# A gated feed-forward kernel whose first x transfers carry one block of 128 columns, whose first matmuls run in halves of 256 tokens, and whose last output piece has 128 columns

## Chip, cores and metric

The kernel runs on one core of a Trainium2 chip. The metric is the time of one execution in microseconds (us) of device time. The profile's own span is about 1.8 us shorter than that time (297.4 against 299.16 us in the profiled run of the kernel before).

## The reference

```python
B, S, D, F = 32, 32, 1024, 3584            # 1024 tokens, all bf16
def reference(x, w_gate, w_up, w_down):
    return (gelu_tanh(x @ w_gate) * (x @ w_up)) @ w_down
```

A "block" below is one of the 8 slices of 128 along D, the dimension that the first two products sum over. A "pair m" is one group of 128 gate columns and 128 up columns of F. The first two products read x with D on the partitions. Of the first 512 tokens, blocks 0 and 1 of x are loaded as they are and transposed on PE. The DMA transposes blocks 2 to 7, and all blocks of the other 512 tokens, on the way.

## The kernel before: the parts that matter

A helper, `pr.add(engine, operation, ..., r=, w=)`, records every operation with the keys that it reads and writes, and makes the waits from them. All operations therefore carry one line number (L98) in the profile, and one reads by the names of the tiles.

```python
# PE: dummy matmuls while the first data is on its way
for n in [512] * 6 + [128] * 2:
    pr.add("pe", "matmul", ps[:, 3, 0:n], one[:, 0:P], one[:, 0:n], ...)
NX = 2
for i, eng in enumerate(("sp", "act")):        # x, blocks 0 and 1: rows of 512 B, 128 KB on each queue
    pr.add(eng, "dma_start", xn[:, 2*i:2*i+2, :], x_r[:, 2*i:2*i+2, 0:NX*P], w=[("xn", i)], dma=f"xn{i}")
for k in range(NX):                            # weights of blocks 0 and 1, pairs 0-3
    load_w("sp", "g", 0, k, k + 1)
    load_w("act", "u", 0, k, k + 1)
for k0, k1 in ((2, 3), (3, 4), (4, 5), (5, 6), (6, 8)):
    load_x(0, k0, k1)                          # DMA transposes, on SP
load_w("act", "g", 0, 2, 4)                    # weights of blocks 2 and 3
load_w("act", "u", 0, 2, 4)
# ... (cut)
for k in range(NX):                            # eight transposes and four copies, before any real matmul
    for i, b in enumerate((6, 7) if k == 0 else (4, 5)):
        half = ps[:, b, 0:P].bitcast(BF16)
        for t in range(2):
            pr.add("pe", "transpose", half[:, t*P:(t+1)*P], xn[:, 2*i+t, k*P:(k+1)*P], ident[:, :], ...)
        pr.add("dve", "tensor_copy", xT[:, k, i*256:(i+1)*256], half, ...)
# ... (cut) then for tokens 0-511: per block k, four gate and four up matmuls of 512 tokens,
#     pair m into PSUM banks 2m (gate) and 2m+1 (up)
# ... (cut) the output, in pieces of (token chunk, column, columns), each copied by ACT or DVE in turn
jobs = [[(tc, 0, 512), (tc, 512, 512)] for tc in range(TC - 1)]
jobs += [[(TC-1, 0, 512)], [(TC-1, 512, 256)], [(TC-1, 768, 256)]]
```

## Time and profile before

| | before |
|---|---|
| time, median of the 3 runs first given | 300.06 us (299.55 to 300.38) |
| span of the profile | 297.4 us |
| PE busy | 292.7 us, 98% |
| first real matmul | 4.61 us |
| block 1's first matmul | 6.33 us |
| last copy out of PSUM starts | 294.96 us |

These are lines from the profile page of the kernel before: the busy time of each engine with its share of the span, and the chain of waits that ended last, by engine.

```profile
PE 292.7 (98%) x1362; PEld 79.3 (27%) x808; DVE 42.5 (14%) x68; ACT 37.5 (13%) x67; POOL 0.7 (0%) x6
PE 98%; issue 0%; ACT 0%
```

PE is the bound, and nearly the whole chain is PE. Little can therefore be won, apart from what happens before PE starts (4.6 us) and after it stops (2.4 us).

This is the timeline of the kernel before at its start. The columns are the start in us, the length of the stretch in us, engine, line, operation, output<-inputs, forms and count. A bracket, where there is one, gives the idle time just before and what ended it.

```profile
3.51 1.06 PE L98 MATMUL ps<-ident,xn 128*128 128x128 bf16 x8
3.96 0.93 DVE L98 COPY xT<-ps 128x256 bf16<-128x256 bf16 x4 [3.96 <-PE ps L98]
4.61 1.02 PE L98 MATMUL ps<-xT,wg 128*128 128x512 bf16 x4
...
6.33 1.03 PE L98 MATMUL ps<-xT,wg 128*128 128x512 bf16 x4
```

Transposes at 3.51 us, copies at 3.96, the first matmul at 4.61. From there a matmul starts every 0.216 us, so eight of them, one block, take 1.73 us. Block 1 starts at 6.33 and block 2 at 8.06 (not shown), without a gap. Before a certain moment PE runs at half this rate: the dummies of 512 columns start 0.427 us apart. That moment is called the clock step below. Here it lies between the last transpose (starts at 4.25, the transposes 0.106 us apart) and the first matmul: the clock record of this trace begins at 4.59 us.

These are the early transfers of the kernel before (output<-input, issuing queue, kind, count, KB, us from issue to landing). The first two were issued at 0.74 us, the third (block 0's gate weights) at 1.26, the fourth (block 1's gate weights) at 1.75, and the last (up weights of blocks 2 and 3) at 2.76.

```profile
xn<-in_x_dram ACTq DMA_DIRECT2D x1, 128.0 KB, 2.9
xn<-in_x_dram SPq DMA_DIRECT2D x1, 128.0 KB, 2.7
wg<-in_w_gate_dram SPq DMA_DIRECT2D x1, 128.0 KB, 2.7
wg<-in_w_gate_dram SPq DMA_DIRECT2D x1, 128.0 KB, 3.8
wu<-in_w_up_dram ACTq DMA_DIRECT2D x1, 256.0 KB, 5.8
```

So x is there at 3.40 and 3.62 us, block 0's gate weights at 4.01 and block 1's at 5.51. (The prediction's 3.44, 3.64 and 3.96 are what the rounded durations give.) The up weights of blocks 2 and 3 are there at 8.60 us; PE uses them at 8.93. This is a supply that keeps just ahead of PE, with 0.3 to 1.3 us to spare for the weights of blocks 0 to 2 and for x of block 2.

These are the shares of the chain of waits of the kernel before within its first 18 us, by line.

```profile
by line: PE ps L98 96.0%; issue 0.8%
```

No DMA stands in it. And this is the end of the kernel before, in the timeline:

```profile
294.96 0.38 ACT L98 ACTIVATE xT<-ps 128x256 bf16<-128x256 f32 x1 [5.52 <-PE ps L98]
295.37 0.33 SPq L98 DMA_DIRECT2D out_dram<-xT  x1
```

The last copy takes 0.38 us for 256 columns. Then comes the issue of the store, and the span ends at 297.38: 2.42 us after the start of that copy.

### The profile page before, as it was taken

To read this page: it belongs to the slowest core of one execution; us is meant where nothing else is said; L and a number is where in the kernel's file an instruction comes from. 1 tells how busy PE (TensorE), PEld (TensorE's weight loads), DVE (VectorE), ACT (ScalarE), POOL (GpSimd) and SP (SyncE) were. 2 spreads that over 40 slices of the span, in tenths; PEclk is the share of its full clock that TensorE was granted. 3 is DMA by queue.
4 is the path that set the end of the run, shared out by engine and by line. 5 is a ranking of instruction groups with operands and counts; after the bars stand their busy time and mean duration, and the time that the engine had idled before them with its cause. 6 is when DMAs were issued, how large, how long until landed. Compare 5 with 4: busy or idle time off the path is not lost.

```text
span 297.4 us, 2549 instructions
## 1 busy us (share of the span) xinstructions
PE 292.7 (98%) x1362; PEld 79.3 (27%) x808; DVE 42.5 (14%) x68; ACT 37.5 (13%) x67; POOL 0.7 (0%) x6
## 2 busy tenths in 40 slices
PE   8999999999999999999999999999999999999996
PEld 4444222222222222222222222222222222222255
DVE  1030311112211111111111221110000000000000
ACT  1030411111111111211111111110000000000010
POOL 0000000000000000000000000000000000000000
PEclk9999999999999999999999999999999999999999
DMA  7999734006608309121030030000101101001011
GB/s 201 268 247 354 237 106 142 1 0 225 198 2 304 121 10 355 62 102 39 0 141 2 0 141 0 0 2 0 35 0 37 35 0 35 15 23 35 0 35 35
DMA packets 28842, 26.37 MB, mean 89 GB/s; under 512 B 8224, under 2 KB 25248, under 8 KB 28832
## 3 DMA queue, kind: packets, MB, share of 16 engines
q1 hardware_dynamic: 26640, 24.25, 25.5%
q10 hardware_dynamic: 2192, 1.97, 2.3%
q8 instruction: 8, 0.13, 0.2%
q14 instruction: 2, 0.02, 0.0%
HBM read 22.28 MB, written 2.10 MB: 82 GB/s over the span
## 4 chain that ended last, share of the span: by engine, by line
PE 98%; issue 0%; ACT 0%
PE ps L98 56%; PE ps L163 43%; ACT xT L98 0%
## 5 line engine op out<-in xcount | busy, mean ns | idle before, releaser
L98 PE MATMUL ps<-xT,wg 128*128 128x512 bf16 x250 | 88.4, 379 | 0.3
L98 PE MATMUL ps<-xT,wu 128*128 128x512 bf16 x250 | 87.9, 379 | 0.2
L98 PE MATMUL ps<-wd,hT 128*128 128x512 bf16 (+1 forms) x272 | 83.6, 357 | 0.0
L163 PE MATMUL ps<-wd,hT 128*128 128x512 bf16 x196 | 74.3, 379 | 0.4
L163 PE MATMUL ps<-xT,wu 128*128 128x512 bf16 x189 | 71.6, 379 | 0.3
L163 PE MATMUL ps<-xT,wg 128*128 128x512 bf16 x189 | 71.6, 379 | 0.2
L98 DVE TENSOR_TENSOR hT<-g,ps 128x512 bf16<-128x512 f32 x56 | 36.3, 685 | 158.1 <-PE ps L98 152.5
L98 ACT ACTIVATE g<-ps 128x512 f32<-128x512 f32 x56 | 30.8, 595 | 159.8 <-PE ps L98 159.8
L98 PEld LDWEIGHTS ps<-wd,hT 128*128 128x128 bf16 x280 | 27.4, 98 | 69.8 <-issue 65.8
L98 PEld LDWEIGHTS ps<-xT,wu 128*128 128x128 bf16 x256 | 25.0, 98 | 71.7 <-issue 64.1
L98 PEld LDWEIGHTS ps<-xT,wg 128*128 128x128 bf16 x256 | 25.0, 98 | 71.5 <-issue 64.0
L98 DVE CAST xT<-ps 128x512 bf16<-128x512 f32 (+1 forms) x8 | 5.3, 658 | 87.7 <-ACT xT L98 79.8
L98 ACT ACTIVATE xT<-ps 128x512 bf16<-128x512 f32 (+1 forms) x9 | 5.2, 573 | 94.6 <-PE ps L98 94.6
L98 PE MATMUL ps<-const-bfloat16-1.0 128*128 128x512 bf16 (+1 forms) x8 | 2.9, 545 | 0.8 <-PEq L309 0.8
L98 ACT ACT_TABLE_LOAD x1 | 1.3, 1283 | 3.5 <-issue 3.5
L98 PEld LDWEIGHTS ps<-const-bfloat16-1.0 128*128 128x128 bf16 x8 | 1.0, 137 | 2.4 <-issue 2.4
L98 DVE COPY xT<-ps 128x256 bf16<-128x256 bf16 x4 | 0.9, 292 | 4.0 <-PE ps L98 4.0
L98 PE MATMUL ps<-ident,xn 128*128 128x128 bf16 x8 | 1.1, 311 | 0.0
L98 PEld LDWEIGHTS ps<-ident,xn 128*128 128x128 bf16 x8 | 0.8, 136 | 0.0
L98 POOL TENSOR_SCALAR_AFFINE_SELECT ident<-ident 128x128 bf16<-128x128 bf16 x1 | 0.3, 295 | 0.2 <-POOL ident L98 0.2
L98 POOL MEMSET ident<- 128x128 bf16 x1 | 0.2, 205 | 0.3 <-POOLq L309 0.3
L98 ACT ACTIVATE warm<-const-float32-0.0 128x1 f32<-128x1 f32 x1 | 0.2, 203 | 0.0
(4 smaller groups left out, 0.4 us busy)
## 6 DMA issues: line engine op xcount, KB each, us to landing
wd<-in_w_down_dram SPq DMA_DIRECT2D x7, 1024.0 KB, 5.1
wg<-in_w_gate_dram SPq DMA_DIRECT2D x6, 1024.0 KB, 7.8
wu<-in_w_up_dram SPq DMA_DIRECT2D x6, 1024.0 KB, 10.1
out_dram<-xT SPq DMA_DIRECT2D x15, 128.0 KB, 1.7
wg<-in_w_gate_dram ACTq DMA_DIRECT2D x3, 256.0 KB, 4.9
wu<-in_w_up_dram ACTq DMA_DIRECT2D x3, 256.0 KB, 5.2
wu<-in_w_up_dram ACTq DMA_DIRECT2D x2, 128.0 KB, 3.8
wg<-in_w_gate_dram SPq DMA_DIRECT2D x2, 128.0 KB, 3.3
```

The source lines that it names most:

```text
L98: ins = name(eng, *args, **kw) if callable(name) else getattr(eng, name)(*args, **kw)
L163: return eng.add_instruction(mybir.InstMatmult(start_tensor_calc=start, stop_tensor_calc=stop, ldweights=False, name=nc.get_next_instructi ...
```

## The change

The intent: PE could start sooner if its first transfer were smaller and its first matmuls needed less of x. So the first x transfers carry only block 0 (64 KB on each queue). Block 0's matmuls of pairs 0 to 2 run on the first 256 tokens while the second 256 are still being copied. Block 1 of x comes in one later transfer, and PE transposes it between two of those halves. One dummy matmul is dropped. The last output piece has 128 columns instead of 256, so that its copy and its store are shorter.

```diff
-for n in [512] * 6 + [128] * 2:
+for n in [512] * 5 + [128] * 2:
...
-    pr.add(eng, "dma_start", xn[:, 2*i:2*i+2, :], x_r[:, 2*i:2*i+2, 0:NX*P], w=[("xn", i)], dma=f"xn{i}")
-for k in range(NX):
-    load_w("sp", "g", 0, k, k + 1)
-    load_w("act", "u", 0, k, k + 1)
+    pr.add(eng, "dma_start", xn[:, 2*i:2*i+2, 0:P], x_r[:, 2*i:2*i+2, 0:P], w=[("xn", i, 0)], dma=f"xn{i}")
+load_w("sp", "g", 0, 0, 1)
+load_w("act", "u", 0, 0, 1)
+pr.add("sp", "dma_start", xn[:, :, P:NX*P], x_r[:, 0:4, P:NX*P], w=[("xn", 0, 1), ("xn", 1, 1)], dma="xn2")
+load_w("act", "g", 0, 1, 2)
+load_w("act", "u", 0, 1, 2)
...
+pe_x(0)                                   # 4 transposes, 2 copies (banks 6 and 7)
+six = [(m, kind) for kind in "gu" for m in range(3)]
+for m, kind in six:
+    mm_gu(kind, m, 0, 0, 2*m + (kind == "u"), quarter=0)     # tokens 0-255
+for m, kind in six:
+    if (m, kind) == (0, "u"):
+        pe_x(1)                           # 4 transposes, 1 copy of 512 (bank 7)
+    mm_gu(kind, m, 0, 0, 2*m + (kind == "u"), quarter=1)     # tokens 256-511
# pair 3 of block 0 follows in full; its up matmul writes bank 7
...
-jobs += [[(TC-1, 0, 512)], [(TC-1, 512, 256)], [(TC-1, 768, 256)]]
+jobs += [[(TC-1, 0, 512)], [(TC-1, 512, 384)], [(TC-1, 896, 128)]]
```

On the queues, this gives the third place on SP, where block 1's gate weights stood, to block 1 of x. The gate weights go to ACT, and everything behind them on ACT moves one issue down.

More of the change, by code (lines that the diff above doesn't have):

```diff
@@ L167, in held_matmul, with mm_gu @@
                 tile_size=(P, P), tile_position=(0, 0)))
-        def mm_gu(kind, m, h, k, bank, w=(), held=False):
+        def mm_gu(kind, m, h, k, bank, w=(), held=False, quarter=None):
             buf, slot = where[m]
             wt = (wg_b if kind == "g" else wu_b)[buf]
-            pr.add("pe", held_matmul if held else "matmul", ps[:, bank, :], wt[:, k, slot * P:(slot + 1) * P], xT[:, k, h * 512:(h + 1) * 512],
-                start=(k == 0), stop=(k == DK - 1),
-                r=[(kind, buf, slot, k), ("x", k, h)] + ([("x", k, "b")] if h == 0 else []), w=[("ps", bank), *w])
+            c0, n = (0, 512) if quarter is None else (256 * quarter, 256)
+            keys = [("x", k, h)] if quarter != 1 else []
+            if h == 0 and quarter != 0:
+                keys.append(("x", k, "b"))
+            kw = {} if h or m > 2 else dict(skip_group_check=True)
+            pr.add("pe", held_matmul if held else "matmul", ps[:, bank, c0:c0 + n],
+                   wt[:, k, slot * P:(slot + 1) * P], xT[:, k, h * 512 + c0:h * 512 + c0 + n],
+                   start=(k == 0 and quarter != 1), stop=(k == DK - 1),
+                   r=[(kind, buf, slot, k), *keys], w=[("ps", bank), *w], **kw)
         glu_n = [0]
@@ L197, in bass_standalone__geglu_ffn__sampling_kernel @@
         for i, eng in enumerate(("sp", "act")):
-            pr.add(eng, "dma_start", xn[:, 2 * i:2 * i + 2, :], x_r[:, 2 * i:2 * i + 2, 0:NX * P], w=[("xn", i)], dma=f"xn{i}")
-        for k in range(NX):
-            load_w("sp", "g", 0, k, k + 1)
-            load_w("act", "u", 0, k, k + 1)
+            pr.add(eng, "dma_start", xn[:, 2 * i:2 * i + 2, 0:P], x_r[:, 2 * i:2 * i + 2, 0:P], w=[("xn", i, 0)], dma=f"xn{i}")
+        load_w("sp", "g", 0, 0, 1)
+        load_w("act", "u", 0, 0, 1)
+        pr.add("sp", "dma_start", xn[:, :, P:NX * P], x_r[:, 0:4, P:NX * P], w=[("xn", 0, 1), ("xn", 1, 1)], dma="xn2")
+        load_w("act", "g", 0, 1, 2)
+        load_w("act", "u", 0, 1, 2)
         def load_x(h, k0, k1, r=()):
@@ L211, in bass_standalone__geglu_ffn__sampling_kernel, with pe_x @@
         pr.add("act", "activation", warm[:, 0:1], const0, ACTF.Gelu_apprx_tanh)
-        for k in range(NX):
-            for i, b in enumerate((6, 7) if k == 0 else (4, 5)):
-                half = ps[:, b, 0:P].bitcast(BF16)
+        def pe_x(k):
+            for i in range(2):
+                b = 6 + i if k == 0 else 7
+                half = ps[:, b, (0 if k == 0 else i * P):(P if k == 0 else (i + 1) * P)].bitcast(BF16)
                 for t in range(2):
                     pr.add("pe", "transpose", half[:, t * P:(t + 1) * P], xn[:, 2 * i + t, k * P:(k + 1) * P],
-                           ident[:, :], r=[("xn", i), "ident"], w=[("ps", b)])
-                pr.add("dve", "tensor_copy", xT[:, k, i * 256:(i + 1) * 256], half, r=[("ps", b)],
-                       w=[("x", k, 0) if i == 0 else ("x", k, "b")])
+                           ident[:, :], r=[("xn", i, k), "ident"], w=[("ps", b)])
+                if k == 0:
+                    pr.add("dve", "tensor_copy", xT[:, k, i * 256:(i + 1) * 256], half, r=[("ps", b)],
+                           w=[("x", k, "b") if i else ("x", k, 0)])
+            if k:
+                pr.add("dve", "tensor_copy", xT[:, k, 0:512], ps[:, 7, 0:256].bitcast(BF16), r=[("ps", 7)],
+                       w=[("x", k, 0)])
+        pe_x(0)
+        six = [(m, kind) for kind in "gu" for m in range(3)]
+        for m, kind in six:
+            mm_gu(kind, m, 0, 0, 2 * m + (kind == "u"), quarter=0)
+        for m, kind in six:
+            if (m, kind) == (0, "u"):
+                pe_x(1)
+            mm_gu(kind, m, 0, 0, 2 * m + (kind == "u"), quarter=1)
         KO = 2
@@ L226, in bass_standalone__geglu_ffn__sampling_kernel @@
                 steps += [(m, kind, k) for kind in "gu" for k in range(KO)] if h else []
-            for k in range(KO if h else 0, DK - KO):
+            if h == 0:
+                steps += [(3, kind, 0) for kind in "gu"]
+            for k in range(KO if h else 1, DK - KO):
                 steps += [(m, kind, k) for kind in "gu" for m in range(4)]
@@ L270, in bass_standalone__geglu_ffn__sampling_kernel @@
         jobs = [[(tc, 0, 512), (tc, 512, 512)] for tc in range(TC - 1)]
-        jobs += [[(TC - 1, 0, 512)], [(TC - 1, 512, 256)], [(TC - 1, 768, 256)]]
+        jobs += [[(TC - 1, 0, 512)], [(TC - 1, 512, 384)], [(TC - 1, 896, 128)]]
         ji = 0
```

## The prediction

> **What bounds the kernel now.** TensorE does. The page gives PE 292.7 us busy of a 297.4 us span (98%), and the chain of waits that ended last is 98% PE. The timeline shows the stream of 512-column matmuls starting one every 0.216 us from 4.61 us, without a gap, to about 294.9 us. Only the ends are left to win: 4.6 us of head and 2.5 us of tail.
>
> *Head (timeline and DMA view).* The two x transfers (128 KB each, issued at 0.74) land at 3.44 and 3.64 us; the dummy matmuls occupy PE until 3.51. Eight transposes follow, 0.106 us apart, four copies run at 3.96 to 4.89 us, and the first real matmul starts at 4.61, just after the second copy (end 4.46). Its weights had landed at 3.96. The dummies (0.43 us each at 512 columns) and the transposes run at half rate; the matmuls from 4.61 run at full rate. [...]
>
> *Tail.* Last matmul ends 294.9, copy on ACT 0.38 us, issue at 295.37, landing 1.6 us later.
>
> **What changes, costed.**
>
> 1. Half the bytes in the first x transfers: landing about 0.35 us earlier (estimate from the 430 KB moved by 3.44 us). One dummy fewer: PE free at about 3.1. Two, not four, transposes and one copy before the first half matmul: it starts near 4.0 us, 0.6 us earlier.
> 2. But it then runs before the clock step, at half rate: 0.5 us of it does 0.25 us of work. Loss 0.25 us.
> 3. The four transposes of block 1 and their copy move into the stream: 0.22 us of PE time. Their copy (512 columns, estimate 0.43 us from the 292 ns copies and the slope of the casts) must end before the up matmul of m=3, which uses the same PSUM bank 7. PE has 0.77 us of work from the start of these transposes, the copy chain needs about 1.0: a stall near 0.2 us. Block 1 of x lands at about 5.2 us (estimate), when PE wants it: 0 to 0.2 us more.
> 4. Halves: 0.109 us each, as the 256-column matmuls of the tail show, so no cost.
>
> Sum: block 1's matmuls start at 6.4 to 6.6 us, against 6.33 before. The head gains nothing, or loses 0.1 to 0.2 us. The weights of blocks 2 and 3, now one issue (0.47 us) later on the ACT queue, had 0.4 to 0.5 us of slack, and should just be in time.
>
> 5. Tail: the copy falls from 0.38 to 0.28 us (slope of the two ACT forms) and the landing by 0.05. Gain 0.15 us if 128-column matmuls run at 0.056 us each. If the weight load (98 ns in the records) limits them, [...]. No run here shows which.
>
> **Predicted:** 300.1 us, range 299.2 to 301.0. Faster by over 2%: 0.01, within 2%: 0.97, slower: 0.02.
>
> **Signs.** Right: first real matmul at 3.9 to 4.1 us with starts 0.21 us apart for halves at first; a PE gap before m=3's up matmul; block 1's matmuls at 6.4 to 6.6; 128-column matmuls 56 ns apart at the end. Wrong: halves at 0.108 us from the start, no gap, block 1 before 6.2.
>
> **What would make it wrong.** The clock step coming later [...]; late block-1 x or weights of blocks 2 and 3; a step before 4 us [...]; weight loads binding in the tail.

The forecast came to 300.1 us, range 299.2 to 301.0. Terms are cut from it where the mark stands, because they rested on figures that no run of this case shows: when the clock step comes and what moves it, what a step at another time would lose or gain, and what weight loads could cost in the tail. The estimate of 5.2 us for block 1 of x stands without the numbers that it came from. The terms that remain give 299.9 to 300.1 us: 300.06 before, 0 to 0.2 us lost in the head, 0.15 us gained in the tail.

## More of the kernel before

Only runs in the fast state are compared. One run in the slow state turned up and is described at the end.

## The result, and the profile after

| | before | after |
|---|---|---|
| time, median of 6 runs each | 299.99 us (299.55 to 300.54) | 300.70 us (300.04 to 301.63) |
| ratio after/before | | 1.0024, 95% interval 1.0004 to 1.0044 |
| span of the profile | 297.4 us | 298.2 us |
| first real matmul | 4.61 us | 4.31 us |
| block 1's first matmul | 6.33 us | 7.26 us |
| last copy starts | 294.96 us | 296.08 us |
| from there to the end of the span | 2.42 us | 2.17 us |

Ratios are the mean time of one kernel's fast runs over that of the other's of the same rounds, so not quite the ratio of the medians quoted. The kernel after is slower by about 0.7 us, a quarter of a per cent.

The same page lines, of the kernel after (busy times; the chain of waits by engine):

```profile
PE 294.2 (99%) x1393; PEld 78.0 (26%) x813; DVE 42.7 (14%) x67; ACT 37.4 (13%) x67; POOL 0.7 (0%) x6
PE 97%; DMA 1%; SPq 0%; ACT 0%; issue 0%
```

A DMA now stands in the chain. The start of the kernel after, in the timeline:

```profile
3.08 0.63 PE L98 MATMUL ps<-ident,xn 128*128 128x128 bf16 x4
3.54 0.51 DVE L98 COPY xT<-ps 128x256 bf16<-128x256 bf16 x2 [3.54 <-PE ps L98]
4.31 0.50 PE L98 MATMUL ps<-xT,wg 128*128 128x256 bf16 x3 [0.60 <-DMA wg<-in_w_gate_dram]
4.81 0.50 PE L98 MATMUL ps<-xT,wu 128*128 128x256 bf16 x3
5.15 0.49 PE L98 MATMUL ps<-xT,wg 128*128 128x256 bf16 x3
6.11 0.40 PE L98 MATMUL ps<-ident,xn 128*128 128x128 bf16 x4 [0.47 <-DMA xn<-in_x_dram]
6.34 0.49 PE L98 MATMUL ps<-xT,wu 128*128 128x256 bf16 x3
6.55 0.42 DVE L98 COPY xT<-ps 128x512 bf16<-128x512 bf16 x1 [2.50 <-PE ps L98]
7.03 0.39 PE L98 MATMUL ps<-xT,wu 128*128 128x512 bf16 x1
7.26 1.03 PE L98 MATMUL ps<-xT,wg 128*128 128x512 bf16 x4
```

PE starts 0.30 us earlier. Three groups of halves follow, the last of which starts at 5.15 us. At about 5.48 PE has issued the last of them (three, 0.109 us apart). The next thing in its order are block 1's transposes, which start at 6.11: PE stood still for 0.63 us. (The bracket gives less, since it counts from the modelled end of the last matmul.) Then the up matmul of pair 3 comes at 7.03, 0.36 us after the matmul before it instead of 0.216: it waited for the copy at 6.55 to leave bank 7. Block 1 begins at 7.26, 0.93 us later than before.

Waits of the kernel after in its first 16 us (engine, tiles <- what it waited for: us in total, times, longest; PEld is PE's loading of weights); before, no such line names a DMA.

```profile
PEld ps L98 <- DMA wu<-in_w_up_dram: 1.1, 3, 0.5
PE ps L98 <- DMA wg<-in_w_gate_dram: 0.6, 1, 0.6
PE ps L98 <- DMA xn<-in_x_dram: 0.5, 1, 0.5
```

And the chain of waits of the kernel after in its first 18 us, first by line, then the piece that matters (start, us, what):

```profile
by line: PE ps L98 67.2%; DMA xn<-in_x_dram 24.0%; SPq L98 5.0%; issue 1.2%
1.75 4.32 DMA xn<-in_x_dram
```

The piece that decides is block 1 of x, 4.3 us under way from its issue at 1.75 us. The early transfers of the kernel after, in the same columns as before (issued at 0.74, 0.74, 1.24, 1.75 and 3.50 us):

```profile
xn<-in_x_dram ACTq DMA_DIRECT2D x1, 64.0 KB, 2.2
xn<-in_x_dram SPq DMA_DIRECT2D x1, 64.0 KB, 2.0
wg<-in_w_gate_dram SPq DMA_DIRECT2D x1, 128.0 KB, 3.0
xn<-in_x_dram SPq DMA_DIRECT2D x1, 128.0 KB, 4.3
wu<-in_w_up_dram ACTq DMA_DIRECT2D x1, 256.0 KB, 6.4
```

Block 0 of x lands at 2.74 and 2.95 us, 0.7 us earlier than x did before. Block 0's gate weights, behind half as many bytes, land no earlier in this profile, at 4.26 us (in the four other profiles of this head at 3.81 to 4.00). Block 1 of x lands at 6.06. The up weights of blocks 2 and 3 land at 9.9 instead of 8.6 us.

The end of the kernel after, in the timeline:

```profile
295.72 0.33 PE L98 MATMUL ps<-wd,hT 128*128 128x128 bf16 x3
296.08 0.28 ACT L98 ACTIVATE xT<-ps 128x128 bf16<-128x128 f32 x1 [5.52 <-PE ps L98]
296.39 0.33 SPq L98 DMA_DIRECT2D out_dram<-xT  x1
```

The last three of the 128-column matmuls start within 0.11 us (0.056 us apart), the copy takes 0.28 us, and the span ends 2.17 us after its start instead of 2.42. The tail is a gain of 0.25 us. The head lost 1.12 us (294.96 to 296.08): the first activation that reads PSUM comes at 15.60 us before and at 16.73 after, and from there to the start of the last copy 279.36 us pass in both. In 13 profiles this stretch is the same within 0.001 us, so what differs between these kernels lies before it or after it.

### The profile page after: what moved, and what is told of

It reads as the page before. It is cut to its first block, busy times and chain, and to the rows that moved or that the text cites. A ratio compares the mean times of both kernels' runs of the same rounds, so it can differ in the third digit from the quotient of the medians.

```text
span 298.2 us, 2585 instructions
## 1 busy us (share of the span) xinstructions
PE 294.2 (99%) x1393; PEld 78.0 (26%) x813; DVE 42.7 (14%) x67; ACT 37.4 (13%) x67; POOL 0.7 (0%) x6
## 2 busy tenths in 40 slices
DMA packets 29370, 26.37 MB, mean 88 GB/s; under 512 B 9392, under 2 KB 25776, under 8 KB 29360
## 4 chain that ended last, share of the span: by engine, by line
PE 97%; DMA 1%; SPq 0%; ACT 0%; issue 0%
PE ps L98 55%; PE ps L163 42%; DMA xn<-in_x_dram 1%; SPq L98 0%; ACT xT L98 0%
## 5 line engine op out<-in xcount | busy, mean ns | idle before, releaser
L98 PE MATMUL ps<-xT,wg 128*128 128x512 bf16 (+1 forms) x259 | 90.5, 377 | 0.6 <-DMA wg<-in_w_gate_dram 0.6
L98 PE MATMUL ps<-xT,wu 128*128 128x512 bf16 (+1 forms) x259 | 90.5, 377 | 0.0
L98 PE MATMUL ps<-wd,hT 128*128 128x512 bf16 (+2 forms) x280 | 86.6, 358 | 0.0
L163 PE MATMUL ps<-xT,wg 128*128 128x512 bf16 x192 | 72.8, 379 | 0.0
L163 PE MATMUL ps<-xT,wu 128*128 128x512 bf16 x192 | 72.8, 379 | 0.0
L98 PEld LDWEIGHTS ps<-wd,hT 128*128 128x128 bf16 x280 | 26.3, 98 | 71.0 <-issue 65.8
L98 DVE COPY xT<-ps 128x256 bf16<-128x256 bf16 (+1 forms) x3 | 0.9, 336 | 6.0 <-PE ps L98 6.0
```

The costliest lines, as they stand in the source:

```text
L98: ins = name(eng, *args, **kw) if callable(name) else getattr(eng, name)(*args, **kw)
L163: return eng.add_instruction(mybir.InstMatmult(start_tensor_calc=start, stop_tensor_calc=stop, ldweights=False, name=nc.get_next_instructi ...
```

## The experiments

Two theories stood against each other. **Supply**: the head is a race between PE and the transfers that feed it; the change made block 1 of x and the weights behind it later, so PE waits, whenever it starts. **Order**: the loss comes from what PE now does, halves and transposes in the stream, a copy to wait for, and half-rate work before the clock step. Twelve runs were made, in four batches: nine new kernels, the tail change alone twice more, and the kernel after once more. Each was timed in 6 executions beside 11 of the kernel before.

### The two parts of the change alone

`tail_only` is the kernel before with one line changed:

```diff
-jobs += [[(TC-1, 0, 512)], [(TC-1, 512, 256)], [(TC-1, 768, 256)]]
+jobs += [[(TC-1, 0, 512)], [(TC-1, 512, 384)], [(TC-1, 896, 128)]]
```

> The kernel before with only the last output piece changed to 384 and 128 columns. Theory: the tail part is a gain of 0.2 to 0.35 us on its own (in the profile after, 2.1 us passed from the start of the last copy to the end of the span against 2.4 before), so a ratio of 0.9990 to 0.9993; the 128-column matmuls start 0.055 us apart. Rival (weight loads bind the 128-column matmuls): [...].

Measured: 299.39 us against 299.83, ratio 0.9982 (0.9970 to 0.9995). That is more than expected, but the expected ratios lie within the interval. Starts of the 128-column matmuls: 0.056 us apart, each with its own weight load (98 ns in the records). So the weight loads do not bind there. The rival's figures are cut, since no run of this case shows them.

`head_only` is the kernel after with that line put back.

> The kernel after with the tail of before, so the head changes alone, and a second look at them. Theory: 0.9 to 1.3 us slower than before (ratio 1.003 to 1.0045), block 1 of x landing at 5.6 to 6.3 us again and PE waiting for it for 0.4 us or more. Rival (that landing was an accident of one execution): block 1 lands by 5.3 us, PE does not wait, the loss is under 0.5 us.

Measured: 301.05 us, ratio 1.0033 (1.0012 to 1.0054), so about 1.0 us lost by the head, as expected. The wait of 0.4 us or more for block 1 of x, also expected, is a miss: PE did not wait for it here. The timeline of `head_only`:

```profile
4.01 0.82 PE L98 MATMUL ps<-xT,wg 128*128 128x256 bf16 x3 [0.31 <-DMA wg<-in_w_gate_dram]
5.78 0.39 PE L98 MATMUL ps<-ident,xn 128*128 128x128 bf16 x4
6.92 1.03 PE L98 MATMUL ps<-xT,wg 128*128 128x512 bf16 x4
...
10.20 0.61 PE L98 MATMUL ps<-xT,wu 128*128 128x512 bf16 x2 [0.53 <-DMA wu<-in_w_up_dram]
```

Here PE ran at half rate from 4.01 to about 5.5 us (half matmuls 0.213 us apart) and therefore met block 1 of x (landed at 5.73) without waiting. Yet block 1's matmuls started at 6.92 us, within the 6.88 to 7.27 of the other profiles of this head. And at 10.20 the up matmuls of block 2 waited for weights that landed at 10.15. The half-rate work and the wait for x fill the same time: they do not add.

### PE's new order on the old transfers

`order_only` is the kernel after with the transfers, dummies and tail of before:

```diff
 # against the kernel after
-(x in 64 KB pieces, block 1 third on SP, block 1's gate weights on ACT; 5 dummies; 384 + 128)
+(x in 128 KB pieces of two blocks, weights alternately on SP and ACT; 6 dummies; 256 + 256)
```

> The kernel before with its own transfers and dummies, but the halves and the late transposes of block 1 as PE does them after. Theory (the loss is made of transfers): no PE wait for a DMA in the first 7 us, block 1's matmuls start at 6.3 to 6.6 us (6.33 before, 7.26 after), total within 0.3 us of before. Rival (the order of work on PE costs the microsecond): block 1's matmuls at 7 us or later and a loss near 1 us.

Measured: 299.79 us against 299.83, ratio 0.9999 (0.9984 to 1.0014). Its timeline:

```profile
4.38 0.49 PE L98 MATMUL ps<-xT,wg 128*128 128x256 bf16 x3 [0.36 <-DMA wg<-in_w_gate_dram]
5.61 0.39 PE L98 MATMUL ps<-ident,xn 128*128 128x128 bf16 x4
6.75 1.03 PE L98 MATMUL ps<-xT,wg 128*128 128x512 bf16 x4
```

Its expectation held for the time; two details missed: PE waited for block 0's gate weights (landed at 4.27 us) and again, for about 0.25 us, for its up weights (4.90), and block 1 started at 6.75, a little late. PE did not wait for block 1 of x. The order of work on PE, including the wait for bank 7 (0.14 us here too), neither gains nor costs more than the interval allows, 0.5 us. `order_only` and `head_only` ran in the same batch and differ in the transfers and one dummy alone; `six_dummies` below loses as much with the dummy put back. The microsecond comes from the transfers.

### Why block 1 of x is late

`x1_both_queues` splits block 1's transfer over both queues and puts block 1's gate weights back on SP:

```diff
-pr.add("sp", "dma_start", xn[:, :, P:NX*P], x_r[:, 0:4, P:NX*P], ...)
-load_w("act", "g", 0, 1, 2)
+for i, eng in enumerate(("sp", "act")):
+    pr.add(eng, "dma_start", xn[:, 2*i:2*i+2, P:NX*P], x_r[:, 2*i:2*i+2, P:NX*P], ...)
+load_w("sp", "g", 0, 1, 2)
```

> The kernel after, but block 1 of x is split over both queues as block 0 is, its two 64 KB transfers third on each, and block 1's gate weights are back on SP. Theory [...] block 1 lands by about 5.2 us instead of 6.05, the PE wait for it falls from about 0.6 us to under 0.2, and the time is 0.4 to 0.7 us below that of after. Rival (block 1 is late because it stands behind the first weights, or the engines are busy): it lands at 5.7 us or later and nothing is won.

Measured: block 1 landed at 4.90 and 5.08 us, and the wait for it was gone. This landing is as expected. And the time was 300.53 us, ratio 1.0016 (1.0002 to 1.0030), against 1.0024 for the kernel after in its own batch: the expected gain of 0.4 to 0.7 us does not show, and the 0.2 us between the two ratios are within the noise. The timeline of `x1_both_queues` shows where the time went:

```profile
4.95 0.46 PE L98 MATMUL ps<-ident,xn 128*128 128x128 bf16 x4
5.93 0.39 PE L98 MATMUL ps<-xT,wu 128*128 128x512 bf16 x1
7.09 1.04 PE L98 MATMUL ps<-xT,wg 128*128 128x512 bf16 x4 [0.77 <-DMA wg<-in_w_gate_dram]
...
9.80 1.02 PE L98 MATMUL ps<-xT,wg 128*128 128x512 bf16 x4 [0.81 <-DMA xT<-in_x_dram]
```

Block 0 was finished 0.18 us ahead of the kernel before: its last matmul started at 5.93, so block 1 could have begun at 6.15. Then PE stood until 7.09 for block 1's gate weights (landed at 7.04), and again until 9.80 for x of block 2 (landed at 9.66). One wait was taken away and the next in line took its place.

`x1_double` is the kernel after with twice the bytes in the late transfer, in as many packets (29370 in the whole execution with either):

```diff
-pr.add("sp", "dma_start", xn[:, :, P:NX*P], x_r[:, 0:4, P:NX*P], ...)
+pr.add("sp", "dma_start", xn[:, :, P:3*P], x_r[:, 0:4, P:3*P], ...)   # block 2 of it is not used
```

> The kernel after with the late x transfer doubled: it carries blocks 1 and 2 (rows of 512 B, 256 KB; block 2 of it is not used). The number of its packets stays, its bytes double. Theory [...]: it lands less than 0.5 us later than after's 5.7 to 6.05 us, so at 6.0 to 6.5 us. Rival [...]: twice the bytes behind the same start need another 0.8 us or more, so 6.7 us or later.

Measured: 300.21 us, ratio 1.0010 (0.9989 to 1.0031); the late transfer landed at 6.08 us, inside the expected 6.0 to 6.5 us. The transfer in its list of DMA issues:

```profile
xn<-in_x_dram SPq DMA_DIRECT2D x1, 256.0 KB, 4.3
```

It took 4.3 us for 256 KB, as after it took 4.3 us for 128 KB (3.9 to 4.3 us in four profiles). Twice the bytes move the landing by 0.4 us at most (6.08 us against 5.69 to 6.06). Each packet record in the trace is one row, and its length on an engine is (256 and 1024 B the same in the traces of before and after, 512 B in that of before):

| row of | packet record, median of the first 12 us |
|---|---|
| 256 B | 18 ns |
| 512 B | 27 ns |
| 1024 B | 46 ns |

Among the first transfers of `x1_double` only this one has rows of 512 B. Its 512 rows moved between 3.59 and 5.23 us. In that stretch SP's queue moved 684 rows in all, ACT's 182 rows of 1024 B: nearly four to one. How the two queues shared the engines, and whether ACT's queue always had rows ready, stays open, since the records do not name the engine. Of the 4.3 us, about 1.85 passed before the first row moved (the rows of block 0's gate weights, ahead on SP, ended at 3.63), 1.64 while the rows moved, and 0.85 from there to the last completion. So the forecast of the landing came true, but as an estimate of the author's: its reason was not shown.

One reading stands in the traces. The third transfer on SP lands that late with either set of transfers. With those of before it is block 1's gate weights, 128 KB in 128 rows of 1024 B. They landed at 5.51, 5.95, 5.63, 5.35 and 6.61 us in the five profiles at the head of the table further down, 5.81 on the mean. Block 1 of x in that place landed at 5.69 to 6.08, 5.87 on the mean, in 512 rows of 256 or of 512 B. The place was as late before as after. But block 1's gate weights are wanted at 6.33, and PE wants block 1 of x when it has issued the last halves before its transposes, at 5.0 to 5.5 us in the four profiles that waited.

`x_small_packets` is the kernel before, but each of its two first transfers takes one block of all four token groups, so that the same 128 KB come in rows of 256 B:

```diff
-pr.add(eng, "dma_start", xn[:, 2*i:2*i+2, :], x_r[:, 2*i:2*i+2, 0:NX*P], ...)
+pr.add(eng, "dma_start", xn[:, :, i*P:(i+1)*P], x_r[:, 0:4, i*P:(i+1)*P], ...)
 # every transpose now waits for both
```

> The kernel before with the same two first transfers of 128 KB, but each takes one block of 128 columns of all four token groups, so rows of 256 B instead of 512. Theory (a 256 B packet keeps an engine 18 ns, a 512 B one 27): x takes 64 packets of 18 ns on each engine instead of 32 of 27, lands 0.3 us later (3.7 to 3.9 us), the first real matmul starts at 4.85 to 5.0 us and the time grows by 0.2 to 0.4 us (ratio 1.0007 to 1.0013). Rival (bytes count, packets don't): x lands at 3.4 to 3.7 us as before, no loss.

Measured: x landed at 3.54 and 3.84 us (3.40 and 3.62 before, 3.50 and 3.78 in `two_halves_tail`, which has the old rows and ran in the same batch), the first matmul started at 4.99 us, and the time was 300.01 us, ratio 0.9994 (0.9972 to 1.0016). The landing moved by at most 0.2 us, less than the 0.3 expected, and no loss was seen. In `g1_on_act`, with the old rows and also in that batch, x landed at 3.64 and 3.87. Inconclusive: rows of 256 B in these two transfers cost 0.2 us of landing at most, and no time that shows.

### The other weights, and the early start

`g1_on_act` is the kernel before with block 1's gate weights issued from ACT:

```diff
-    load_w("sp", "g", 0, k, k + 1)
+    load_w("sp" if k == 0 else "act", "g", 0, k, k + 1)
```

> The kernel before with one transfer moved: block 1's gate weights are issued from ACT, so that the up weights of block 1 and the weights of blocks 2 and 3 come one issue (about 0.5 us) later on ACT, as after. Theory (the head is a race of transfers with PE, and the later weight issues lose it): PE waits for weights of blocks 1 to 3 for 0.3 to 0.8 us, ratio 1.001 to 1.003. Rival [...]: no more waits than before, ratio under 1.001.

Measured: 300.24 us, ratio 1.0008 (0.9981 to 1.0034), inconclusive in time. In its profile the up weights of blocks 2 and 3 landed at 10.34 us, 0.3 us after PE wanted them, although PE was late too, since the clock step came at 6.66 us in that execution. This run does not settle what the moved issue alone is worth, and the rival's reason is cut, since it was not shown.

`six_dummies` is the kernel after with the sixth dummy put back, which takes away the early start; `after_again` is the kernel after, unchanged, in the same batch.

> The kernel after once more, unchanged, for a second profile of it and as the measure of the next run, on the same chip. Theory: ratio to before 1.002 to 1.004 with the tail's gain in it; PE waits for block 1 of x, or comes to it late because the clock step was late; block 1's matmuls start at 6.8 to 7.3 us.

> The kernel after with the sixth dummy matmul put back, so that PE reaches the first transposes and the first half matmuls about 0.4 us later. Theory (PE only waits for block 1 of x and later weights, so the early start is worth nothing): the same time as after_again within 0.2 us, block 1's matmuls again at 6.8 to 7.3 us. Rival (the early start is worth its 0.4 us and something else lost more): 0.3 to 0.5 us slower than after_again.

Measured: `after_again` 300.29 us, ratio 1.0031 (1.0004 to 1.0059); `six_dummies` 300.56 us, ratio 1.0029 (1.0004 to 1.0053). The timeline of `six_dummies`:

```profile
4.39 0.49 PE L98 MATMUL ps<-xT,wg 128*128 128x256 bf16 x3 [0.26 <-DVE xT L98]
5.74 0.40 PE L98 MATMUL ps<-ident,xn 128*128 128x128 bf16 x4 [0.20 <-DMA xn<-in_x_dram]
6.88 0.59 PE L98 MATMUL ps<-xT,wg 128*128 128x512 bf16 x2
```

The first half matmul starts at 4.39 instead of 3.97 us, and block 1 at 6.88 instead of 6.99. By the ratios, starting 0.4 us later costs nothing that shows (each interval is 0.7 us or more to either side, so the times alone do not exclude 0.4 us). The profiles say why: PE only stands that much less before block 1 of x (landed at 5.69; 5.80 in `after_again`).

### All heads side by side

Landings are the last of the 16 completions of a transfer, and the columns are in us from the start of the span. The last column is the first activation that reads PSUM. It comes once pair 0 of all 8 blocks is done, and what follows up to the last copy takes 279.36 us in every profile, so it sums up the head. `x1_both_queues`, `g1_on_act` and `x_small_packets` have transfers of their own and are left out (first activation at 17.33, 17.14 and 17.48 us).

| profile | first matmul | block 1 of x landed | block 1 starts | up weights of blocks 2, 3 landed | first activation |
|---|---|---|---|---|---|
| *transfers of before* | | | | | |
| before | 4.61 | 3.62 | 6.33 | 8.60 | 15.60 |
| tail_only | 4.61 | 3.53 | 6.33 | 9.36 | 16.09 |
| tail_third | 4.69 | 3.52 | 6.44 | 9.19 | 16.03 |
| order_only | 4.38 | 3.36 | 6.75 | 8.78 | 16.01 |
| two_halves_tail | 4.44 | 3.78 | 6.66 | 10.07 | 17.10 |
| *transfers of after* | | | | | |
| after | 4.31 | 6.06 | 7.26 | 9.94 | 16.73 |
| after_again | 3.97 | 5.80 | 6.99 | 9.83 | 17.32 |
| head_only | 4.01 | 5.73 | 6.92 | 10.15 | 18.06 |
| six_dummies | 4.39 | 5.69 | 6.88 | 9.82 | 17.07 |
| x1_double | 4.04 | 6.08 | 7.27 | 9.85 | 16.68 |

On the mean, the first activation comes at 16.17 us in the upper group and at 17.17 in the lower: the 1.0 us that `head_only` lost in the timed runs. Block 1 starts at 6.50 and at 7.06 us, so 0.56 us of it is gone by then. In four of the five lower profiles PE waited for block 1 of x; in `head_only` half-rate matmuls filled that time. The other 0.44 us is lost later, in waits for weights and for x of the following blocks. The up weights of blocks 2 and 3 are an example. They land 0.72 us later in the lower group (9.92 against 9.20), but PE wants them 2.59 us after block 1 starts (twelve matmuls of 0.216 us) and is itself 0.56 us later. They come up to 0.6 us too late in four of the five lower profiles. In the upper group they come 0.4, 0.2 and 0.8 us too late in `tail_only`, `tail_third` and `two_halves_tail`. So the old transfers have no slack there either, and these ten profiles do not single out one later transfer as the cause of the 0.44 us. One profile of a kernel is one draw: the landing of the same transfer moves by up to 1.5 us between the profiles of one group, and the times of one kernel spread over 0.7 to 2.7 us.

### Versions meant to beat both

`two_halves_tail` keeps the old transfers and early transposes, runs only the first two gate matmuls in halves, and has the new tail. Its core:

```diff
+for half in range(2):
+    for m in range(2):
+        mm_gu("g", m, 0, 0, 2*m, half=half)      # then the other matmuls of block 0 in full
```

> A candidate: the kernel before with its transfers, dummies and early transposes, the 384 and 128 tail, and only the first two gate matmuls of block 0 in halves, so that PE starts after the first copy. Expected: first real matmul at 4.4 us instead of 4.61, no wait for a copy, time 0.3 to 0.7 us below before (ratio 0.9977 to 0.9990); if the transfers bound the head, as the theory has it, the 0.2 us of the start are lost again at blocks 1 to 3 and it equals the tail change alone (0.9982).

Measured: first matmul at 4.44 us, time 299.71 us, ratio 0.9991 (0.9969 to 1.0012). The earlier start shows in the profile, but no gain over the tail alone.

The tail alone ran twice more.

> The tail change alone once more. Theory: 0.2 to 0.6 us below before again (ratio 0.998 to 0.9993); from the start of the last copy to the end of the span 2.05 to 2.2 us against 2.4. Rival: the gain of 0.5 us seen first was chance, ratio 1.000.

> The tail change alone a third time, since the first two gave 0.9982 and 0.9998 and the second has one execution in a very slow state (447 us) that its profile fell in. Theory: a gain of 0.3 us, the difference that the profiles show after the last matmul (ratio 0.999), which one such run of six executions cannot tell from nothing; from the start of the last copy to the end of the span 2.05 to 2.2 us. Rival: no gain in the profile, 2.4 us.

Measured: ratios 0.9998 (0.9978 to 1.0018, its slow execution left out) and 0.9976 (0.9954 to 0.9999). The last copy in `tail_third`:

```profile
295.38 0.28 ACT L98 ACTIVATE xT<-ps 128x128 bf16<-128x128 f32 x1 [5.52 <-PE ps L98]
```

Its span is 297.57 us, so 2.19 us from there to the end, against 2.42 before. Over all fast profiles it is 2.14 to 2.19 us with the new tail, and 2.34 to 2.42 with the old: 0.23 us on the means, seen every time. The three ratios average 0.9985, or 0.4 us; two of the three intervals leave out 1. Since this change leaves the head as it was, what the ratios show beyond 0.23 us is best put down to the scatter of the heads. The tail change alone is the version that beats both kernels: the kernel before by 0.23 us, the kernel after by about 1 us (0.7 and 0.23).

## Why the prediction was right, point by point

The prediction said 300.1 us (299.2 to 301.0), within 2%; measured were 300.7 us. The measured time lies inside the range, which is 1.8 us wide. The change that it forecast was next to nothing (300.1 against 300.06 us: up to 0.2 us lost in the head, 0.15 gained in the tail), and 0.7 us were lost. So there is luck in it: two landings in the head came later than forecast, and the range was wide enough to hold them. The prediction had named both, "late block-1 x or weights of blocks 2 and 3", among what would make it wrong. Term by term:

- **The bound and where to look: right.** Only the two ends changed.
- **PE starts near 4.0 us: right within the scatter.** Profiles of this head with five dummies show 3.97, 4.01, 4.04 and 4.31 us. In the last, block 0's gate weights held it up by about 0.3 us, which the prediction had not foreseen.
- **"it then runs before the clock step, at half rate ... Loss 0.25 us": a matter of chance.** In four profiles of this head it came both ways: in `head_only` and `x1_double` the first halves were 0.213 us apart, in `after` and `after_again` 0.11 from the start, which the prediction had listed as a sign of its being wrong. It also does not add to the loss, since PE would have waited for block 1 of x anyway.
- **"Block 1 of x lands at about 5.2 us ..., when PE wants it: 0 to 0.2 us more": the step that was mis-sized.** PE wanted it at 5.0 to 5.5 us, about as forecast, but it landed at 5.7 to 6.1. PE stood for 0.6 us (after) or 0.8 us (after_again). The prediction does not say how it came to 5.2. The profile of the kernel before could have told better: what stood in that place, third on SP, had landed at 5.51 us.
- **"a stall near 0.2 us" for bank 7: right.** It was 0.14 us, and the copy took 0.425 us, as estimated from the slope (0.43). `order_only` has the same stall and loses nothing measurable.
- **Halves cost nothing: right,** 0.109 us each.
- **Block 1 at 6.4 to 6.6 us: wrong,** 6.9 to 7.3, because of block 1's landing.
- **The weights of blocks 2 and 3 "should just be in time", with 0.4 to 0.5 us of slack: the slack was mis-sized.** Their issue moved by 0.74 us (2.76 to 3.50), their landing by 0.7 us in the means. They were up to 0.6 us too late in four of five profiles, although PE came later as well. But the slack read from one profile was a lucky draw: with the old transfers they were late in three of five profiles. About 0.4 us of the head's loss falls after block 1's start, and which transfer it belongs to stays open.
- **Tail, gain 0.15 us if the 128-column matmuls run at 0.056 us: right, a little small.** They run at 0.056 us and the gain is 0.23 us.

The head lost about 1.0 us (`head_only`, ratio 1.0033) and the tail gave back 0.23. That leaves about 0.8 us; measured were 0.7 us, and 0.9 in the batch of `after_again`.

## What to carry to other kernels

When PE's start is fed by transfers that arrive just ahead of it, starting PE earlier can be lost again at the next transfer that does not arrive earlier too; look for the smallest slack among the next few transfers before moving the first. To guess when a transfer will land in a new place of a queue, read from the profile what landed in that place before: here 5.51 us, and in one profile only, so look at several if you can. Moving a transfer that is wanted early into a late place makes a wait, even if the place itself gets no later (0.6 us in after, 0.8 in after_again). A change at the tail of the kernel, where nothing follows, is kept in full (0.23 us in every profile), while one at the head has to survive every later wait.

## What else the traces show

- The 28 matmuls of 128 columns at the end of the kernel after, each with its weight load (98 ns in the records), started 0.056 us apart; those of 256 columns at the end of the kernel before 0.109 us.
- The clock records of these traces, where there is one, put the step to the full rate at 3.73 (`x1_both_queues`), 4.49, 4.59 (before), 4.74, 5.07, 5.20, 5.66 and 6.66 us (`g1_on_act`), so 2.95 to 5.9 us after the first dummy at 0.78 us.
- The packet records are 18, 27 and 46 ns for rows of 256, 512 and 1024 B. If their length grows evenly with the bytes, about 9 ns are fixed, half of the time of a 256 B row: an estimate from these three numbers.
- In the third place on SP, 128 KB in 1024 B rows took 3.6 to 4.9 us from issue to landing, 128 KB in 256 B rows 3.9 to 4.3 us, and 256 KB in 512 B rows 4.3 us, beside 1024 B rows on the other queue.
- The run in the slow state: one execution of `tail_again` took 447 us instead of 299. Its matmuls of 512 columns started 0.29 and 0.36 us apart in turn, so 0.32 on the mean, one and a half times 0.216. ACT and DVE took their usual times (595 ns for an activation and 685 ns for a product of 512 columns, as in `tail_only`), so PE alone was slow. The trace holds no clock record, so the clock of 1.000 below is no measurement. The line of cores (us, granted clock) and three lines of the timeline of that profile:

```profile
core 0: 445.7 us, clock 1.000
199.74 0.52 PE L98 MATMUL ps<-xT,wu 128*128 128x512 bf16 x1
200.03 0.52 PE L163 MATMUL ps<-xT,wu 128*128 128x512 bf16 x1
200.38 0.52 PE L98 MATMUL ps<-xT,wu 128*128 128x512 bf16 x1
```

What slowed it is open. It was left out of all ratios.
